# Another form of seven products in gate/up and feature transform, and one more product made jointly

## The chip, the cores and the metric

The kernel runs on one core of a Trainium2 chip. The metric is the device time of one execution in microseconds (us), taken as the median of several runs. Five engines work side by side, each through its own stream of instructions in order: TensorE (PE in the profile; PEld is its weight load), VectorE (DVE), ScalarE (ACT), GpSimd (POOL), which here only starts transfers, and SyncE (SP), which starts most of the loads. Transfers run on 16 DMA engines. TensorE adds up its results in eight PSUM banks.

## The reference

The input x has 2048 rows of 512 in float32. Two branches are mixed by a gate g, one number a row.

```python
# A: the real part of a two-dimensional Fourier transform, by matrices
a = einsum("bsd,ed->bse", x, dft_hid_re)
b = einsum("bsd,ed->bse", x, dft_hid_im)
A = einsum("ts,bse->bte", dft_seq_re, a) - einsum("ts,bse->bte", dft_seq_im, b)
# B: a gated unit with 1792 hidden features
gate = einsum("bsd,df->bsf", x, W_gate)
up   = einsum("bsd,df->bsf", x, W_up)
B = einsum("bsf,fd->bsd", gate * (gate > 0) * up, W_down)

g = sigmoid((x * gate_w).sum(-1, keepdims=True))
return g * A + (1 - g) * B
```

## The kernel before

**Products.** Every float32 operand is split into a high and a low part: ScalarE casts it to the high part (names ending in h), VectorE subtracts that from the original for the low part (ending in l). A product of two matrices is then three matmuls: high by low, low by high, high by high (`PARTS`). On top of that, 2 x 2 block products are done with seven half-size products instead of eight (Strassen, or Winograd's form of it), so the operands of a product are sums of blocks, made by VectorE, and the results are sums of products, made in PSUM or by VectorE and ScalarE.

**Two forms of seven products.** `LEFT`, `RIGHT`, `ORDER` and `BANK` (lines 25 to 30) describe the form that the gate/up blocks (`Block`, line 560) and the feature transform (`SpectralBlock`, line 734) use before: order 5, 2, 1, 3, 4, 6, 7 in three pairs of banks a, b, c. In `Block` bank c is begun by ScalarE with minus the content of a ("seed"), and product 1 is added on top; the other sums are made by VectorE on the way out. The stages `Round`, `Down`, `Sequence` and `Joint` use the other form already, in which banks called A, B (or E), X, D and G are begun by copies of other banks.

**Stages**, in the order of TensorE, where the plan's time is counted in "keys", one key for one matmul of 128 x 128 x 512:

1. `Direct`: the first block of gate/up without the form of seven, 96 keys; then 11 `Block`s of 84 keys. A `Block` makes 256 hidden features, gate and up, for one half of the rows (q). Its weights are prepared by `Weights`; its result h and sums of it are stored by `h_out` for later.
2. Four `SpectralBlock` stages of 84 keys (the two feature transforms, real and imaginary), with the last two `Block`s behind them.
3. `Down`, twice 294 keys: the down projection for both halves.
4. The sequence transform: a real matrix (m = 0) and an imaginary one (m = 1), each for two halves of the output rows (p). `Sequence(left, m, p)` makes those products that are not in `JOINT`, product by product, each in four parts (jj) of 12 matmuls. `Joint(m, of)` makes one product of the outer form for both halves of the columns and rows at once, with another level of the form of seven inside: seven products, each in two parts of 6 matmuls. `JOINT` before holds (0, 1), (0, 2), (0, 3) and (1, 2): matrix and outer product.

The stages of m = 0 leave their results in the scratch tensor zd; those of m = 1 begin from it: `Sequence.fill` loads z and ScalarE copies it into a bank before the products come. In each `Sequence` of m = 1 before, bank A is filled with z11, product 1 is added, VectorE makes bank B from z12 minus A (`seed`), and the later products are added there.

**Operands of the sequence transform.** `right_sums` loads four blocks of a transform matrix (tiles p), makes four sums on VectorE and stores them to the scratch tensor tb through GpSimd's queue. The table `SUMS` says which (matrix, outer product or 4 + p, part) are done so, and at which key; of 4 and 5 stand for the two `Sequence` halves. Joint stages and those parts of `Sequence` read the sums back (tiles jr and r from tb). Other parts load three blocks, make three sums on the spot and get the fourth by an accumulating transfer through GpSimd's queue. The tiles ch, cl (in joint stages jch, jcl) are the split right operands; lh, ll (jt) the split left ones.

**What sets the order.** All of this is written as steps with a key, and `Plan` orders them before the kernel is built: it models each step's length and each transfer, works out when each must be done (due), and lists the steps of each engine in the order in which they would start. VectorE's and ScalarE's steps go by due time and may not begin more than 40 keys ahead of their key. Buffers are 51 units of 4 KB per partition; a step whose unit isn't free yet has to wait. In the kernel on the chip every engine and queue then runs its list in order. PSUM banks are handed out in rotation, eight in all.

Of the kernel before, what the change touches and what calls it, by code (L numbers as in the profile page):

```python
# [24 lines left out]
LEFT = {1: ("11", "22", 1), 2: ("21", "22", 1), 3: ("11",), 4: ("22",), 5: ("11", "12", 1),  # L25
        6: ("21", "11", -1), 7: ("12", "22", -1)}
RIGHT = {1: ("11", "22", 1), 2: ("11",), 3: ("12", "22", -1), 4: ("21", "11", -1), 5: ("22",),
         6: ("11", "12", 1), 7: ("21", "22", 1)}
ORDER = (5, 2, 1, 3, 4, 6, 7)
BANK = {5: "a", 3: "a", 6: "a", 2: "b", 4: "b", 7: "b", 1: "c"}  # L30
# [59 lines left out]
class Step:  # L90


    def __init__(self, key, engine, name, a, k):
# [13 lines left out]
        if name == "tensor_copy":  # L107
            self.work = 0.1 + n * 0.52e-3
            self.hold = self.work - 0.05
        elif name == "dma_start":  # L110
            n = max(x.size() // (P if x.base.kind == "dram" else 1) for x in (*self.writes, *self.reads))
            self.work = n * 4 * P / 4096 * 0.160 / 16 * (2 if "accum_op" in k else 1)
        elif engine == "tensor":
            self.work = self.hold = 0.22667 * n / N
        elif engine == "vector":

            self.work = 0.163 + n * 1.0625e-3
            self.hold = self.work - 0.083
        else:
            self.work = 0.19 + n * 0.845e-3  # L120
            self.hold = self.work - 0.09
# [8 lines left out]
class Queues:  # L130
# [31 lines left out]
    def add(self, step, start):  # L162
# [5 lines left out]
        packets = max(1.0, step.work / (0.160 / 16 * (2 if "accum_op" in step.k else 1)))  # L168
# [176 lines left out]
def kernel(ctx: ExitStack, tc, xP, xG, wf, wgu, wd, cr, ci, wri, gw, out):  # L345
# [40 lines left out]
    wb = hbm("wb", 8, P, 4, 2, P)  # L386
# [61 lines left out]
    def x_raw(q, m):  # L448

        a, *r = RIGHT[m]  # L450
        raw = piece[q, {6: "12", 7: "21"}[m] if m in (6, 7) else a] if not r or m in (6, 7) else buf(f"xs{m}")
        X[q, m] = buf(f"xh{m}", dtype=F32R), buf(f"xl{m}", dtype=F32R), raw

    def x_sum(q, m):
        a, *r = RIGHT[m]
        if m == 6:
            E().vector.scalar_tensor_tensor(X[q, m][2].all, piece[q, a].all, -1.0, piece[q, r[0]].all,
                                            op0=OP.mult, op1=OP.subtract)
        elif r:
            combine(X[q, m][2].all, piece[q, a].all, piece[q, r[0]].all, r[1])  # L460
# [16 lines left out]
    SLOT = {5: 0, 1: 1, 2: 2, 7: 0, 3: 1, 4: 2, 6: 3}  # L477

    class Weights:
        def __init__(self, c):  # L480
            self.c = c
            self.raw = [buf(f"wr{i}", [4, 2, P]) for i in range(2)]
            self.sum = [buf(f"ws{i}", [3, 2, P]) for i in range(2)]
            self.a = [[buf(f"wa{i}{x}", [3, 2, P], F32R) for x in "hl"] for i in range(2)]
            self.b = [[buf(f"wb{i}{x}", [4, 2, P], F32R) for x in "hl"] for i in range(2)]

        def load(self, i):
            load(self.raw[i].all, wgu[self.c, i])

        def a_sum(self, i):  # L490
            r, o = self.raw[i], self.sum[i]
            E().vector.tensor_add(o[:, 0:3], r[:, 0:3], r[:, 1:4])
            E().scalar.copy(self.a[i][0].all, o.all)

        def a_lo(self, i):
            E().vector.tensor_sub(self.a[i][1].all, self.sum[i].all, f32(self.a[i][0].all))

        def b_sum(self, i):
            r = self.raw[i]
            E().vector.tensor_sub(r[:, 0:4:3], r[:, 0:2], r[:, 2:4])  # L500

        def b_hi(self, i):
            E().scalar.copy(self.b[i][0].all, self.raw[i].all)

        def b_lo(self, i):
            E().vector.tensor_sub(self.b[i][1].all, self.raw[i].all, f32(self.b[i][0].all))

        def keep(self, key):
            for n, t in enumerate(y for x in (self.a, self.b) for i in x for y in i):
                k = t.shape[0]  # L510
                op(key + 3 * n, lambda n=n, t=t, k=k: store(wb[n, :, :k], f32(t.all)))

        def fetch(self, key):
            for n, t in enumerate(y for x in (self.a, self.b) for i in x for y in i):
                k = t.shape[0]
                op(key + 6 * n, lambda n=n, t=t, k=k: load(f32(t.all), wb[n, :, :k]))

        def of(self, m, i):
            return [t[:, SLOT[m]] for t in (self.a if m in (5, 1, 2) else self.b)[i]]

    def w_prep(w, key, ahead=66):
        for i in range(2):
            op(key - ahead + 6 * i, w.load, i)
            op(key - 36 + 12 * i, w.a_sum, i)
            op(key - 30 + 12 * i, w.a_lo, i)
            op(key + 6 * i, w.b_sum, i)
            op(key + 6 * i, w.b_hi, i)
        op(key + 6, w.b_lo, 0)
        op(key + 12, w.b_lo, 1)
# [30 lines left out]
    class Block:  # L560


        def __init__(self, q, w):
            self.q, self.w = q, w
            self.t, self.g, self.u = buf("t"), buf("g"), buf("u")
            self.h = [buf(f"h{d}") for d in range(2)]
            self.ps = {k: Pair("c") for k in "abc"}
            for m in ORDER:
                for i in range(2):
                    pe(6, self.product, m, i)  # L570
                    self.evac(m, i, plan.now)
            h_out(q, w.c, self.h, plan.now + (8 if plan.now > 270 else 100))

        def product(self, m, i):
            w, x, ps = self.w.of(m, i), X[self.q, m], self.ps[BANK[m]]
            if m in (5, 2) and i == 0:
                ps.new()
            n = 0
            for k in range(2):
                for a, b in PARTS:  # L580
                    mm(ps[i], w[a][:, k], x[b][:, k], start=m in (5, 2) and n == 0, stop=n == 5)
                    n += 1

        def evac(self, m, i, key):
            a, b, c = (self.ps[k] for k in "abc")
            t, g, h = self.t, self.g, self.h

            def go():
                e = E()
                if m == 5:  # L590

                    if i == 0:
                        c.new()
                    e.scalar.activation(c[i], a[i], AF.Copy, scale=-1.0)
                elif m == 2:
                    e.scalar.copy(t[:, i], b[i])
                elif m == 1:
                    e.vector.tensor_sub(t[:, i], c[i], t[:, i])

                elif m in (3, 4):  # L600
                    j, ps = (0, a) if m == 3 else (1, b)
                    if i == 0:
                        e.scalar.activation(g[:, j], ps[0], AF.Relu)
                    else:
                        e.vector.tensor_mul(h[0][:, 1] if m == 3 else h[1][:, 0], g[:, j], ps[1])
                else:
                    j, ps, o = (0, a, h[1][:, 1]) if m == 6 else (1, b, h[0][:, 0])
                    u = self.u[:, j] if i == 0 else o
                    e.vector.tensor_add(u, ps[i], t[:, i])
                    if i:  # L610
                        e.vector.scalar_tensor_tensor(o, self.u[:, j], 0.0, o, op0=OP.max, op1=OP.mult)

            op(key, go)
# [99 lines left out]
    class Spectral:  # L713
# [8 lines left out]
        def prep(self, m, key):  # L722
            a, *r = LEFT[m]
            raw = self.raw[a] if not r or m in (6, 7) else buf(f"vs{m}")
            w = self.w[m] = buf(f"vh{m}", dtype=F32R), buf(f"vl{m}", dtype=F32R), raw
            if r:
                if m == 6:

                    a, r = r[0], (a, -1)
                op(key, lambda a=a, r=r: combine(raw.all, self.raw[a].all, self.raw[r[0]].all, r[1]))  # L730
# [3 lines left out]
    class SpectralBlock:  # L734
        def __init__(self, sp, q, ih):
            self.sp, self.q, self.ih = sp, q, ih
            self.t = buf("t")
            self.o = {b: buf("a" + b, (2, 2, HD)) for b in ("12", "21", "22", "11")}
            self.ps = {k: Pair("a") for k in "abc"}
            for m in ORDER:  # L740
# [3 lines left out]
                if m in (3, 4, 6, 7):  # L744
                    op(plan.now + 3, self.out, {3: "12", 4: "21", 6: "22", 7: "11"}[m])

        def product(self, m, i):
            x, w, ps = X[self.q, m], self.sp.w[m], self.ps[BANK[m]]
            first = m in (5, 2, 1)
# [9 lines left out]
        def evac(self, m, i):  # L759
            e, t = E(), self.t[:, i]  # L760
            a, b, c = (self.ps[k][i] if self.ps[k].banks else None for k in "abc")

            o = self.o[{3: "12", 4: "21", 6: "22", 7: "11"}[m]][:, :, i] if m in (3, 4, 6, 7) else None
            if o:
                a, b, t = (x and x.rearrange("p (k n) -> p k n", k=2) for x in (a, b, t))
            if m == 5:
                e.scalar.copy(t, a)
            elif m == 2:
                e.vector.tensor_add(t, t, b)
            elif m == 1:  # L770
                e.vector.tensor_sub(t, c, t)
            elif m == 3:
                e.scalar.copy(o, a)
            elif m == 4:
                e.scalar.activation(o, b, AF.Copy, scale=-1.0)
            elif m == 6:
                e.vector.scalar_tensor_tensor(o, a, -1.0, t, op0=OP.mult, op1=OP.subtract)
            elif m == 7:
                e.vector.tensor_add(o, b, t)
# [184 lines left out]
    class Sequence(Round):  # L964
        HI, LO = 31, 24

        def __init__(self, left, m, p):
            self.m, self.p, self.early = m, p, 0 if m else 40
            self.ORDER = tuple(x for x in ((1, 7, 6, 5, 4, 3) if m else (1, 5, 6, 7, 4)) if (m, x) not in JOINT)
            self.NEW = () if m else (1, 5, 7)  # L970
            if m:
                self.g = gate_row((2 * p, 2 * p + 1), plan.now + 10)
                self.z = {b: buf("z") for b in ("11", "22", "12")}
                for b, key in zip(self.z, (76, 110, 60)):
                    op(plan.now - key + 48 * (b != "11"), lambda b=b: load(self.z[b].all, zd[self.place(b)]))
# [16 lines left out]
        def rights(self):  # L992
# [5 lines left out]
            for jj in range(4):  # L998
# [9 lines left out]
                for b, t in (("12", 110), ("22", 105), ("11", 90 if m else 100)):  # L1008
                    x = (1 if b == "11" else 7) if m else 5
# [462 lines left out]
```

## Time and profile before

| | before |
|---|---|
| time, median of 3 runs | 783.41 us (783.38 to 784.32) |
| profiled execution, first to last instruction (its span) | 782.1 us |
| TensorE busy | 777.5 us, 3428 matmuls |
| VectorE busy | 698.4 us, 795 instructions |
| ScalarE busy | 406.2 us, 537 instructions |
| moved by DMA | 248.41 MB, 318 GB/s in the mean |

The profiled execution has no time of its own beside its span; the runs' times also hold what lies around the span. Busy time of an engine is the time in which any instruction of it ran. A matmul lasts longer than the distance to the next one, since they overlap; the distance is what counts for a sum. The helper `Step.run` records every operation, so all rows have the same line, L127; groups are told apart by the names of tiles. The DMA share is the time that packets took, as a share of 16 engines, and can pass 1.

### The profile page before, as it was taken

How to read it: one execution, taken by the hardware profiler on the slowest of the kernel's cores; microseconds unless marked ns; L12 is line 12 of the kernel's file. 1: busy time of each engine (PE TensorE's matmuls, PEld its weight loads, DVE VectorE, ACT ScalarE, POOL GpSimd, SP SyncE). 2: the span in 40 equal slices, each digit the busy share in tenths (PEclk: the TensorE clock that was granted, in tenths of full speed). 3: DMA queues.
4: the chain of work that ended last, by engine and by line, in shares of the span. 5: the costliest groups of instructions: out<-in, count | busy, mean ns of one | idle time of the engine just before them, and what ended most of it. 6: DMA issues, size and time to landing. Idle time of an engine off the chain costs nothing.

```text
span 782.1 us, 9936 instructions
## 1 busy us (share of the span) xinstructions
PE 777.5 (99%) x3428; PEld 644.0 (82%) x3428; DVE 698.4 (89%) x795; ACT 406.2 (52%) x537; POOL 115.2 (15%) x181
## 2 busy tenths in 40 slices
PE   9999999999999999999999999999999999999998
PEld 7888888888888888888888888888888888888886
DVE  6999999999999654899997799987999999989896
ACT  5643322222234112464656576576679857645762
POOL 0101322232222112011110000100100002012010
PEclk9999999999999999999999999999999999999999
DMA  8623999999996699589999999989999998997954
GB/s 318 259 95 121 324 404 414 418 325 419 419 396 199 230 338 419 219 302 382 415 417 408 380 313 359 310 281 343 331 390 412 410 358 206 325 238 217 327 156 108
DMA packets 71891, 248.41 MB, mean 318 GB/s; under 512 B 8224, under 2 KB 8992, under 8 KB 71840
## 3 DMA queue, kind: packets, MB, share of 16 engines
q1 hardware_dynamic: 47360, 159.02, 54.1%
q0 software_dynamic: 24336, 88.62, 33.6%
q8 instruction: 27, 0.44, 0.2%
q14 instruction: 24, 0.20, 0.1%
q10 hardware_dynamic: 144, 0.13, 0.1%
HBM read 165.94 MB, written 81.80 MB: 317 GB/s over the span
## 4 chain that ended last, share of the span: by engine, by line
PE 99%; ACT 0%; issue 0%; DVE 0%; ACTq 0%
PE z L127 45%; PE c L127 35%; PE a L127 10%; PE jB L127 3%; PE jA L127 3%; PE jX L127 1%; PE jD L127 1%; PE jG L127 1%; PE warm L127 0%; PE jH L127 0%; ACT jo L127 0%; DVE warm L127 0%; ACTq L127 0%
## 5 line engine op out<-in xcount | busy, mean ns | idle before, releaser
L127 PE MATMUL z<-ch,ll 128*128 128x512 f32 x516 | 200.7, 389 | 0.0
L127 PE MATMUL z<-cl,lh 128*128 128x512 f32 x516 | 200.7, 389 | 0.0
L127 PE MATMUL z<-ch,lh 128*128 128x512 f32 x516 | 200.7, 389 | 0.0
L127 PEld LDWEIGHTS z<-ch,lh 128*128 128x128 f32 x516 | 96.9, 188 | 20.2
L127 PEld LDWEIGHTS z<-ch,ll 128*128 128x128 f32 x516 | 96.9, 188 | 20.0
L127 PEld LDWEIGHTS z<-cl,lh 128*128 128x128 f32 x516 | 96.9, 188 | 20.0
L127 ACT CAST ch<-r 128x1024 fp32r<-128x1024 f32 x80 | 82.5, 1053 | 57.3 <-DVE r L127 43.1
L127 DVE TENSOR_TENSOR cl<-r,ch 128x1024 fp32r<-128x1024 f32 x80 | 96.3, 1220 | 8.2 <-ACT ch L127 6.4
L127 DVE TENSOR_TENSOR cl<-hr,ch 128x1024 fp32r<-128x1024 f32 (+1 forms) x56 | 60.1, 1087 | 11.8 <-ACT ch L127 7.5
L127 DVE TENSOR_TENSOR jcl<-jr,jch 128x1024 fp32r<-128x1024 f32 x56 | 67.2, 1221 | 3.4 <-PE z L127 1.5
L127 ACT CAST ch<-hr 128x1024 fp32r<-128x1024 f32 (+1 forms) x56 | 52.0, 945 | 31.6 <-DMA hr<-hd 11.1
L127 ACT CAST jch<-jr 128x1024 fp32r<-128x1024 f32 x56 | 57.7, 1054 | 5.3 <-DVE jcl L127 2.5
L127 DVE TENSOR_TENSOR p<-p,p 128x1024 f32<-128x1024 f32 x44 | 53.4, 1220 | 0.3
L127 DVE TENSOR_TENSOR r<-r,r 128x1024 f32<-128x1024 f32 x39 | 47.0, 1219 | 3.5 <-DMA r<-cr 3.5
L127 ACT ACTIVATE c<-c 128x512 f32<-128x512 f32 x26 | 15.1, 582 | 66.8 <-PE c L127 66.8
L127 ACT COPY z<-z 128x512 f32<-128x512 f32 x56 | 31.6, 586 | 21.2 <-PE z L127 18.7
L127 PE MATMUL c<-xh,wb0l 128*128 128x512 f32 x104 | 40.5, 389 | 0.0
L127 PE MATMUL c<-xl,wb0h 128*128 128x512 f32 x104 | 40.5, 389 | 0.0
L127 PE MATMUL c<-xh,wb0h 128*128 128x512 f32 x104 | 40.5, 389 | 0.0
L127 PE MATMUL c<-xh,wb1l 128*128 128x512 f32 x104 | 40.5, 389 | 0.0
L127 PE MATMUL c<-xl,wb1h 128*128 128x512 f32 x104 | 40.5, 389 | 0.0
L127 PE MATMUL c<-xh,wb1h 128*128 128x512 f32 x104 | 40.5, 389 | 0.0
(237 smaller groups left out, 1541.1 us busy)
## 6 DMA issues: line engine op xcount, KB each, us to landing
tb<-p POOLq DMA_DIRECT2D x44, 512.0 KB, 10.1
hr<-hd SPq DMA_DIRECT2D x42, 512.0 KB, 9.2
p<-cr SPq DMA_DIRECT2D x36, 512.0 KB, 7.7
jr<-tb SPq DMA_DIRECT2D x32, 512.0 KB, 9.1
hd<-hs POOLq DMA_DIRECT2D x28, 512.0 KB, 8.1
r<-ci SPq DMA_DIRECT2D x24, 512.0 KB, 8.7
l<-ad SPq DMA_DIRECT2D x20, 512.0 KB, 8.7
jr<-cr SPq DMA_DIRECT2D x18, 512.0 KB, 8.8
```

The source lines that it names most:

```text
L127: getattr(getattr(nc, self.engine), self.name)(*map(ap, self.a), **{k: ap(x) for k, x in self.k.items()})
```

## The change

- `Block` and `SpectralBlock` take the form of seven products that the later stages use, in the order 1, 5, 6, 2, 7, 3, 4, with five pairs of banks A, B, X, D, G. ScalarE begins X from A (negated in `Block`), D from X and G from D; it copies B to y and X to s; VectorE adds these to banks B and D on the way out. The weights of gate and up are laid out so that one tile holds both, and their sums and splits follow the new form.
- Product 1 of matrix 1 goes into a joint stage with product 1 of matrix 0: `Joint((0, 1), 1)` runs over four parts (both matrices, two each) and adds all of them up in the same banks. Both `Sequence` stages of m = 1 lose product 1; what they need of it comes in z11 from zd, and z12 minus z11 is made by VectorE ahead of the stage and copied into bank B by ScalarE.
- `SUMS` gets 16 entries instead of 11, at other keys: the two parts of (1, 1) and four more parts of the `Sequence` stages of m = 1 are added, one of m = 0 is taken out.
- The plan's model of transfers takes 0.166 for 0.160 and an accumulating transfer as 1.6 instead of 2 plain ones.

```diff
-ORDER = (5, 2, 1, 3, 4, 6, 7)
-BANK = {5: "a", 3: "a", 6: "a", 2: "b", 4: "b", 7: "b", 1: "c"}
+ORDER = (1, 5, 6, 2, 7, 3, 4)
+BANK = {1: "A", 2: "A", 5: "B", 3: "B", 6: "X", 7: "D", 4: "G"}
...
-            self.work = n * 4 * P / 4096 * 0.160 / 16 * (2 if "accum_op" in k else 1)
+            self.work = n * 4 * P / 4096 * 0.166 / 16 * (1.6 if "accum_op" in k else 1)
...
     def w_prep(w, key, ahead=66):
...
+        for n in range(2):
+            op(key - ahead + 6 * n, w.load, n)
+        for m, n, k in ((None, 0, -40), (5, None, -36), (6, 2, -30), (7, 1, -12), (3, 3, 0)):
+            if m:
+                op(key + k, w.sum, m)
+            if n is not None:
+                op(key + k + 2, w.hi, n)
+                op(key + k + 8, w.lo, n)
...
-    JOINT = ((0, 1), (0, 2), (0, 3), (1, 2))
-    SUMS = {(0, 5, 0): 420, (0, 3, 0): 485, (0, 3, 1): 550, (0, 1, 0): 615, (0, 1, 1): 680, (0, 2, 0): 745,
-            (0, 2, 1): 810, (1, 2, 0): 875, (1, 2, 1): 940, (0, 5, 1): 1640, (0, 4, 1): 1720}
+    JOINT = ((0, 1), (0, 2), (0, 3), (1, 1), (1, 2))
+    SUMS = {(0, 5, 0): 160, (0, 3, 1): 150, (0, 1, 1): 330, (1, 2, 0): 465, (0, 1, 0): 535, (1, 5, 2): 637, (0, 5, 1): 680, (1, 1, 1): 715, (0, 2, 1): 790, (0, 3, 0): 955, (1, 1, 0): 995, (1, 2, 1): 1150, (0, 2, 0): 1270, (1, 5, 1): 1564, (1, 5, 3): 1929, (1, 4, 0): 377}
...
     class Block:
...
+        def evac(self, m, i):
+            e, p, h = E(), self.ps, self.h
+            def seed(k, j, scale=1.0):
+                if i == 0:
+                    p[k].new()
+                e.scalar.activation(p[k][i], p[j][i], AF.Copy, scale=scale)
+            if m == 1:
+                seed("X", "A")
+            elif m == 5:
+                e.scalar.copy(self.y[:, i], p["B"][i])
+            elif m == 6:
+                seed("D", "X")
+                e.scalar.copy(self.s[:, i], p["X"][i])
+            elif m == 7:
+                seed("G", "D")
+            if m in (2, 4):
+                o, ps = (h[0][:, 0], p["A"]) if m == 2 else (h[1][:, 0], p["G"])
+                if i == 0:
+                    e.scalar.activation(self.g[:, m // 4], ps[0], AF.Relu)
                 else:
+                    e.vector.tensor_mul(o, self.g[:, m // 4], ps[1])
+            elif m in (3, 7):
+                o, ps, t = (h[0][:, 1], p["B"], self.s) if m == 3 else (h[1][:, 1], p["D"], self.y)
+                e.vector.tensor_add(t[:, 0] if i == 0 else o, ps[i], t[:, i])
+                if i:
+                    e.vector.scalar_tensor_tensor(o, t[:, 0], 0.0, o, op0=OP.max, op1=OP.mult)
...
     class Sequence(Round):
...
-            self.NEW = () if m else (1, 5, 7)
+            self.NEW = () if m else (5, 7)
...
-                for b, key in zip(self.z, (76, 110, 60)):
+                for b, key in zip(self.z, (76, 110, 98)):
                     op(plan.now - key + 48 * (b != "11"), lambda b=b: load(self.z[b].all, zd[self.place(b)]))
-                for k, b, key in (("A", "11", -14), ("D", "22", 20)):
+                op(plan.now - 16, lambda: combine(self.z["12"].all, self.z["12"].all, self.z["11"].all, -1))
+                for k, b, key in (("D", "22", -14), ("B", "12", -6)):
                     op(plan.now + key, self.fill, k, self.z[b])
             super().__init__(left, (2, 2, 2, 2))
+            if m:
+                self.o["11"] = self.z["11"]
+                self.done("11", self.base + 40)
...
-            if x == 1:
-                op(key, seed)
-                op(key + 1, lambda: both(copy, o["11"], a))
-                self.done("11", key + 6)
...
     class Joint:
...
-        def __init__(self, m, of, last=False):
+        def __init__(self, ms, of, last=False):
...
-            self.lefts(self.base - (60 if last else 80), 10)
-            for jj in range(2):
-                self.rights(jj)
+            for n, m in enumerate(ms):
+                self.lefts(m, self.base - (60 if last else 80) + 4 * n, 10 * len(ms))
+            for j in self.parts:
+                self.rights(*j)
...
-                    for jj in range(2):
-                        pe(6, self.product, x, jj)
+                    for j in self.parts:
+                        pe(6, self.product, x, j)
...
-    Joint(0, 3)
-    for x, key in zip((1, 7, 6, 5, 4, 3), (30, 80, 376, 410, 450, 490)):
+    Joint((0,), 3)
+    for x, key in zip((7, 6, 5, 4, 3), (80, 376, 410, 450, 490)):
...
     Sequence(lefts[0], 0, 1)
-    Joint(0, 1)
-    Joint(0, 2)
+    Joint((0, 1), 1)
+    Joint((0,), 2)
     Sequence(lefts[1], 1, 1)
     Sequence(lefts[1], 1, 0)
-    Joint(1, 2, True)
+    Joint((1,), 2, True)
```

More of the change, by code (lines that the diff above doesn't have):

```diff
@@ L481, in __init__ @@
             self.c = c
[L482 to L506, printed above, removed]
+            self.raw = [buf(f"wr{n}", [4, 2, P]) for n in range(3)] + [buf("wr3", [2, 2, P])]
@@ new lines, in __init__, with load, sum @@
+            self.w = [[buf(f"w{n}{x}", [4, 2, P], F32R) for x in "hl"] for n in range(3)]
+            self.w3 = buf("w3", [4, 2, P], F32R)
+        def load(self, n):
+            load(self.raw[n].all, wgu[self.c, n])
+        def sum(self, m):
+            x, y, z, v = self.raw
+            o, a, b = {5: (z[:, :2], y[:, 2:], y[:, :2]), 7: (y[:, 2:], x[:, :2], y[:, 2:]),
+                       6: (z[:, 2:], z[:, :2], x[:, :2]), 3: (v.all, x[:, 2:], z[:, 2:])}[m]
+            (E().vector.tensor_add if m == 5 else E().vector.tensor_sub)(o, a, b)
@@ L508, in keep, with part, hi, lo @@
+        def part(self, n, x):
+            return self.w[n][x].all if n < 3 else self.w3[:, 2 * x:2 * x + 2]
+        def hi(self, n):
+            E().scalar.copy(self.part(n, 0), self.raw[n].all)
+        def lo(self, n):
+            E().vector.tensor_sub(self.part(n, 1), self.raw[n].all, f32(self.part(n, 0)))
+        def parts(self):
+            return [y for x in self.w for y in x] + [self.w3]
         def keep(self, key):
[L509 to L511 removed]
+            for n, t in enumerate(self.parts()):
+                op(key + 3 * n, lambda n=n, t=t: store(wb[n], f32(t.all)))
@@ L513, in fetch @@
         def fetch(self, key):
-            for n, t in enumerate(y for x in (self.a, self.b) for i in x for y in i):
-                k = t.shape[0]
-                op(key + 6 * n, lambda n=n, t=t, k=k: load(f32(t.all), wb[n, :, :k]))
+            for k, n in enumerate((0, 1, 4, 5, 2, 3, 6)):
+                op(key + 6 * k, lambda n=n: load(f32(self.parts()[n].all), wb[n]))
         def of(self, m, i):
-            return [t[:, SLOT[m]] for t in (self.a if m in (5, 1, 2) else self.b)[i]]
+            n, f = SLOT[m]
@@ L521, in w_prep @@
+            return [(self.w[n][x] if n < 3 else self.w3)[:, 2 * f + i + (2 * x if n == 3 else 0)] for x in range(2)]
     def w_prep(w, key, ahead=66):
[L522 to L529, printed above, removed]
-    JOINT = ((0, 1), (0, 2), (0, 3), (1, 2))
@@ L580, in product @@
                 for a, b in PARTS:
-                    mm(ps[i], w[a][:, k], x[b][:, k], start=m in (5, 2) and n == 0, stop=n == 5)
+                    mm(ps[i], w[a][:, k], x[b][:, k], start=m in (1, 5) and n == 0, stop=n == 5)
                     n += 1
[L584 to L605, printed above, removed]
-                else:
[L607 to L613, printed above, removed]
@@ L1175, in new, with product @@
             self.b[k] = Buf(plan, "j" + k, [N], kind="bank")
-        def product(self, x, jj, k=None, columns=slice(None)):
-            first = x in ((1, 7, 5, 4) if self.last else (1, 5)) and jj == 0 and k is None
+        def product(self, x, j, k=None, columns=slice(None)):
+            begin, end = j == self.parts[0], j == self.parts[-1]
+            first = x in ((1, 7, 5, 4) if self.last else (1, 5)) and begin and k is None
             k = k or {1: "A", 2: "A", 7: "D", 6: "X", 4: "G"}.get(x, "B")
@@ L1181, in product @@
                 self.new(k)
-            c = self.c[x, jj]
+            c, t = self.c[x, *j], self.t[x, j[0]]
             for i in range(2):
                 for n, (a, b) in enumerate(PARTS):
-                    mm(self.b[k][:, columns], self.t[x][:, a, 2 * jj + i], c[b][:, i, columns],
-                       start=first and i == n == 0, stop=jj == i == 1 and n == 2)
+                    mm(self.b[k][:, columns], t[:, a, 2 * j[1] + i], c[b][:, i, columns],
+                       start=first and i == n == 0, stop=end and i == 1 and n == 2)
         def halves(self, h):
-            for jj in range(2):
-                self.product(4, jj, f"H{h}", HALVES[h])
+            for j in self.parts:
+                self.product(4, j, f"H{h}", HALVES[h])
         def evac_on(self, x, key):
```

141 lines of the change are left out of this document (68 added, 73 removed).

## The prediction

> **What bounds the kernel now.** First the page and the list of who waited for whom on TensorE.
>
> ```profile
> span 782.1 us, 9936 instructions
> PE 777.5 (99%) x3428; PEld 644.0 (82%) x3428; DVE 698.4 (89%) x795; ACT 406.2 (52%) x537; POOL 115.2 (15%) x181
> DMA packets 71891, 248.41 MB, mean 318 GB/s; under 512 B 8224, under 2 KB 8992, under 8 KB 71840
> PE warm L127 <- DVE warm L127: 1.1, 1, 1.1
> ```
>
> TensorE's only listed wait is 1.1 us at the start. So the span is a count of matmuls, and only two things can move it: another count, or a first wait. The chain of waits, in order of time, gives the price of a matmul and the stages.
>
> ```profile
> 237.13 76.16 PE a L127 x336
> ...
> 528.17 2.72 PE jA L127 x12
> ...
> 547.21 43.52 PE z L127 x192
> 590.73 2.72 PE jA L127 x12
> ...
> 609.77 2.72 PE jA L127 x12
> ...
> 626.09 2.72 PE jG L127 x12
> 628.81 130.56 PE z L127 x576
> ```
>
> 43.52 / 192 = 0.2267 us a matmul. The feature transform's four stages (a tiles) end at 237.13 + 76.16 = 313.3. Joint stages (j tiles) start at 528.17, 590.73 and 609.77; 84 matmuls make one, 19.04 us. The 576 of z are the two Sequence stages of the second matrix, 288 each. Next the busy time stage by stage, cut at these times; columns: window, length, then busy time and count on PE, PEld, DVE, ACT, POOL, the granted clock, DMA share, GB/s.
>
> ```profile
> 27.69:46.73 19.04, 19.04 (x85) 15.77 (x85) 19.00 (x23) 10.59 (x14) 1.59 (x3) 1.00 0.23 91
> 199.05:218.09 19.04, 19.04 (x85) 15.77 (x85) 17.74 (x21) 4.59 (x7) 5.11 (x9) 1.00 1.03 420
> 418.01:484.65 66.64, 66.64 (x295) 55.20 (x295) 57.57 (x55) 44.23 (x55) 2.13 (x4) 1.00 0.96 366
> 484.65:528.17 43.52, 43.52 (x193) 36.05 (x193) 40.50 (x41) 28.17 (x36) 5.36 (x8) 1.00 0.89 290
> 528.17:547.21 19.04, 19.04 (x85) 15.77 (x85) 14.05 (x13) 13.13 (x18) 0.53 (x1) 1.00 0.94 346
> 547.21:590.73 43.52, 43.52 (x193) 36.05 (x193) 43.18 (x44) 32.53 (x41) 4.56 (x6) 1.00 1.04 366
> 590.73:609.77 19.04, 19.04 (x85) 15.77 (x85) 18.95 (x22) 19.04 (x26) 0.59 (x2) 1.00 1.03 410
> 609.77:628.81 19.04, 19.04 (x85) 15.77 (x85) 18.48 (x20) 15.41 (x23) 1.45 (x3) 1.00 1.02 409
> 628.81:694.09 65.28, 65.28 (x289) 54.07 (x289) 61.48 (x57) 41.70 (x52) 7.33 (x9) 1.00 0.96 283
> 694.09:759.37 65.28, 65.28 (x289) 54.07 (x289) 59.85 (x59) 41.91 (x52) 7.68 (x9) 1.00 0.86 244
> ```
>
> Behind a perfect TensorE three others are nearly full from 547 to 629 us: DVE 80.6 of 81.6 us, ACT all of 19.04 in the first joint stage there, and the DMA share above 1. A full DMA reads 1.02 to 1.04 in this view, so I take 1.03 as its capacity.
>
> **The change, part by part.**
>
> *Matmuls.* A Sequence stage of the second matrix spends 4 x 12 = 48 matmuls on each product (288 / 6). Product 1 leaves both: minus 96. The joint stage for output 1 now has four parts of 6 matmuls for each of seven products, 168 where it had 84: plus 84. Net minus 12, times 0.2267: **minus 2.72 us**. The other form of seven products has the same matmul count in every block. This is the one term on the path.
>
> *Blocks (13) and feature transform (4 stages).* Of each Block's evacuations, DVE has 8 instructions for 10 and ACT 12 for 6; of each transform stage's, DVE 4 for 8 and ACT 14 for 6. One of each kind, with its mean:
>
> ```profile
> L127 DVE TENSOR_TENSOR t<-c,t 128x512 f32<-128x512 f32 x26 | 17.4, 684 | 0.3 <-ACT wa0h L127 0.3
> L127 ACT ACTIVATE c<-c 128x512 f32<-128x512 f32 x26 | 15.1, 582 | 66.8 <-PE c L127 66.8
> ACT c L127 <- PE c L127: 66.8, 23, 7.6
> ACT ch L127 <- DVE r L127: 43.1, 23, 4.4
> L127 ACT CAST jch<-jr 128x1024 fp32r<-128x1024 f32 x56 | 57.7, 1054 | 5.3 <-DVE jcl L127 2.5 <-DVE jr L127 1.1 <-DVE jt L127 0.6
> ```
>
> DVE loses 13 x 2 + 4 x 4 = 42 x 0.684 = 28.7 us; ACT gains 13 x 6 + 4 x 8 = 110 x 0.58 = 64 us, and had 376 us idle. The new waits are seeds: ACT copies bank A into X, X into D, D into G, and a later product adds on top. From a half-product's last matmul to the first matmul that needs its seed lie three other half-products, 18 x 0.2267 = 4.08 us, as for the one seed (c from a) that each Block has already; behind a late seed stand all later matmuls, since TensorE takes them in order, and on ACT the next weight casts. Cost nothing as long as ACT is free within 3.5 us. Five pairs of banks instead of three go round in eight, so a block's second A bank waits for DVE's reading of the last block's first B bank; 24 x 0.2267 = 5.44 us lie between, against 4.08 us for today's tightest DVE read. Bounds: 0 to some 2 us a miss; no gain is possible, for TensorE does not wait there. I take 0. The weights' and x's splits change by a few DVE instructions, less in all; they are covered as the present ones are.
>
> *Block sums written ahead.* There are 16 such groups for 11, each of 4 loads, 4 DVE sums and 4 stores on POOL's queue, and they begin at key 150 instead of 420, where the DMA share is 0.23.
>
> ```profile
> L127 DVE TENSOR_TENSOR p<-p,p 128x1024 f32<-128x1024 f32 x44 | 53.4, 1220 | 0.3
> tb<-p POOLq DMA_DIRECT2D x44, 512.0 KB, 10.1
> 591.96 0.69 DVE L127 TENSOR_TENSOR jn<-jl,jl 128x512 f32<-128x512 f32 x1
> 592.57 4.69 DVE L127 TENSOR_TENSOR jcl<-jr,jch 128x1024 fp32r<-128x1024 f32 x4
> ...
> 619.56 1.22 DVE L127 TENSOR_TENSOR jcl<-jr,jch 128x1024 fp32r<-128x1024 f32 x1
> 620.70 3.49 DVE L127 TENSOR_TENSOR cl<-r,ch 128x1024 fp32r<-128x1024 f32 x3
> ```
>
> Instructions overlap: three take 3.49, so a wide one costs DVE (3.49 - 1.22) / 2 = 1.135 us, a 512-wide one 0.61 (592.57 - 591.96). Five groups more: 20 x 1.135 = 22.7 us of DVE, paid by the 28.7 freed, and 40 transfers, 21.0 MB. Loads go on SP's queue, past weight loads due every second block; stores on POOL's, ahead of the h stores that the Down stages read far later. Cost 0 while they fit the early hole; if not, see the second rival.
>
> *The joint stage with both matrices.* Today's joint stage needs of DVE 14 jcl x 1.135 + 11 left sums and splits x 0.61 + 2 additions x 0.61 = 23.8 us in 19.04, so it eats a lead of 4.8. With both matrices: 28, 22 and 2, 46.4 us in 38.08. The rise is 22.6 us of DVE against 19.04 of TensorE: 3.6 us of lead more. What is there? The last jcl of today's pair ends at 619.56 + 1.22 = 620.78 and is first read half way through the jG product, at 626.09 + 1.36 = 627.45: 6.7 us. 3.1 would be left, and the 5.0 us that DVE idles from 528 to 547 can be drawn on. ACT is alike: 28 casts for 14, with 11.0 us idle from 547 to 591. Stall 0; bounds 0 to 3.6 + (what is lost of 6.7).
>
> Behind it, the second matrix's stages lose 8 cl and 2 left splits, and for four of eight parts the 3 sums made on the spot: 22 x 1.135 = 25 us off DVE. The wait for product 1 and its DVE seed is replaced by a load of z, one subtraction and fills by ACT ahead of the stage. One part of the first matrix goes back to sums on the spot: 3.4 us of DVE where 3.0 are idle and 5.0 follow.
>
> *DMA from 484.65 to 759.37.* Share times length: 38.7 + 17.9 + 45.3 + 19.6 + 19.4 + 62.7 + 56.1 = 259.7 us. Queues from 628.81 to 694.09, then the DMA row in 40 slices from 694.09 to 759.37:
>
> ```profile
> q1 hardware_dynamic: 3965, 13.69, 54.3%
> q0 software_dynamic: 1296, 4.72, 41.6%
> DMA  9989950863499997999999999999999999558500
> ```
>
> A plain 0.524 MB costs 0.524 x 0.543 x 65.28 / 13.69 = 1.36 us; q0's nine, nearly all accumulating, 27.2 / 9 = 3.0 us. Added: 14 jr and 2 jl loads, less 2 left loads: 14 x 1.36 = 19.0. Four parts take 5 loads for 3 and an accumulation: 4 x (2 x 1.36 - 3.0) = -1.1. The part that goes back: 3.0 - 1.36 = +1.6. Sum 279.2; capacity 1.03 x 272.0 = 280.2. But the last six slices leave 6.0 us idle (0.5, 0.5, 0.2, 0.5, 1 and 1 of 1.63), since the last stage's data is in by then. So 5.0 us must go ahead of 484.65, where the stage from 418.01 has (1.03 - 0.96) x 66.64 = 4.7. It fits, barely. I take 0.
>
> The traffic grows by 40 x 0.524 = 21.0 MB for the sums, 14 x 0.524 = 7.3 for these loads and 4 x 0.524 = 2.1 for the four parts: 248.4 + 30.4 = 278.8 MB. The row from 199.05 has 420 GB/s for a whole stage, and at that rate this is 664 us; the rest of the span is room for accumulations.
>
> A rule of the Trainium skill speaks against the change: "DMA: Bandwidth & Descriptors", section Bandwidth, says that a core's share of HBM, about 358 GB/s, binds HBM-SBUF transfers, and not the fabric at 435. By that page my estimate for the same traffic would be 779 us of DMA. The rows from 199.05, 590.73 and 609.77, at 409 to 420 GB/s, do not agree with it.
>
> **The sum.** 782.1 - 2.72 = 779.4 of span. The median lies 783.41 - 782.1 = 1.31 above the profiled span; kept, this gives 783.41 - 2.72 = **780.7 us**. About 0.2% (1.6 us) is what a measurement of this kernel can tell from no change, so faster means under 781.8 and slower above 785.0.
>
> **The rivals.**
>
> *The vector engine's lead is used up.* For: DVE is 99% busy for 81.6 us ahead of 629, and the change asks 22.6 us more in a stretch 19.04 longer. Against: the 6.7 us of lead. If that lead and the 1.0 us idle are all there is, and 6.7 cannot be used because buffers (51 units of 4 KB, of which two matrices' left sides hold about twice as many) keep casts from running ahead, TensorE waits 22.6 - 19.04 - 1.0 = 2.6 us: 783.3, no change.
>
> *The DMA becomes the bound in the last third* (the slower side). Place: 531 to 757 us, where SP's queue is in order, so that one late load holds all behind it. If nothing goes ahead of 484.65, the wait is 279.2 + 6.0 - 280.2 = 5.0 us: 785.7; with capacity 1.00 instead of 1.03 it is 13.2: 793.9. It decides once more than 2.7 us of transfers come too late, and is slower above 4.3. For: four stages read 1.02 to 1.04 already. Against: today DMA in those stages brings r loads for 629 onward, so it runs well ahead.
>
> *Seeds come late.* ACT stood up to 4.4 us behind one DVE result; such a stand plus a cast of 1.05 and the seed of 0.58 would miss 4.08 by 1.95 us. Three such misses in 13 blocks give 786.6. Against: the 4.4 was in a stage of r tiles, and the first seed of each Block has had the same 4.08 without one wait.
>
> *Memory does not sustain the rate.* If the added traffic pulled the mean of the program down to the 366 GB/s of the row from 547.21, 278.8 MB would take 762 us, and with a last joint stage of 19.04 and the end, 3.7, in which nothing is left to load, 784.5 + 1.3 = 785.8. Against: that row holds accumulating transfers, and plain stages read 409 and more. By the Trainium skill's page named above, with 358, it would be 803 as an estimate.
>
> That the change does not remove the 12 matmuls can be excluded: they are counted from its loops.
>
> **How the numbers follow.** Forecast 780.7: 0.61. Vector lead 783.3: 0.12. DMA bound from 785.7: 0.18. Late seeds: 0.07, in part under 785.0 and a little still faster. Memory rate: 0.02. Faster 0.62, same 0.14, slower 0.24. The range begins at 780.2 (the forecast and the lowest of the runs) and reaches to 787.0, into the DMA case; 2 in 10 are left out, mostly above.
>
> **What would show it.** Right: 3416 matmul records, no new row among TensorE's waits, seven joint products of 5.44 us between 591 and 629, Sequence stages of 54.4 us each. The DVE lead at the end of the following joint stage should be near 3 us. Wrong: TensorE waiting for jcl near 640 (first rival), for loads through casts after 629 (second), or for X, D or G banks between 28 and 313 (third). A DMA share that still has holes at 30 to 85 us would say that the early sums did not fill them.

## The result and the profile after

| | before | after |
|---|---|---|
| time, median of 18 runs each | 783.57 us (782.73 to 784.75) | 784.72 us (783.97 to 786.90) |
| ratio to before | | 1.0017 (95% interval 1.0010 to 1.0024) |
| matmuls | 3428 | 3416 |
| span of the profiled run | 782.1 us | 785.0 us |

The 12 matmuls are gone, and yet the kernel is 0.17% slower. The profiled run after is one of four among the 18 that took 786.5 to 786.9 us with a mean granted clock of 0.997 or 0.998, where the other fourteen lie at 784.0 to 785.3; what sets them apart is seen below.

The page of the changed kernel, and behind it its list of TensorE's waits (who waited for whom: us in total, times, longest):

```profile
span 785.0 us, 10154 instructions
PE 777.0 (99%) x3416; PEld 642.2 (82%) x3416; DVE 684.4 (87%) x773; ACT 466.1 (59%) x653; POOL 122.8 (16%) x197
DMA packets 80213, 278.83 MB, mean 355 GB/s; under 512 B 9120, under 2 KB 9888, under 8 KB 80160
```

```profile
PE c L123 <- ACT c L123: 2.5, 1, 2.5
PE warm L123 <- DVE warm L123: 1.1, 1, 1.1
PE z L123 <- ACT z L123: 0.3, 1, 0.3
PE z L123 <- DVE cl L123: 0.2, 1, 0.2
```

There is one new wait of size: once, for an instruction of ScalarE that writes a bank c from a bank c, a seed. TensorE's busy time is longer than 3416 matmuls need (777.0, where 777.5 - 2.72 = 774.8 was to be expected), so some matmuls were slow as well. TensorE in order of time shows both:

```profile
33.73 0.39 PE L123 MATMUL c<-xh,w2h 128*128 128x512 f32 x1
36.62 0.53 PE L123 MATMUL c<-xh,w2l 128*128 128x512 f32 x1 [2.50 <-ACT c L123]
36.95 0.62 PE L123 MATMUL c<-xl,w2h 128*128 128x512 f32 x1
37.37 0.63 PE L123 MATMUL c<-xh,w2h 128*128 128x512 f32 x1
...
39.93 0.59 PE L123 MATMUL c<-xb21h,w0h 128*128 128x512 f32 x1
40.36 0.40 PE L123 MATMUL c<-xb21h,w0l 128*128 128x512 f32 x1
```

Between the starts at 33.73 and 36.62 lie 2.89 us where 0.23 is the rule: 2.66 lost. The next nine steps, to 40.36, take 3.74 us instead of 2.04: another 1.70. The row of that stretch in the view by windows has the granted clock in the column before the DMA share:

```profile
36.62:40.36 3.74, 3.74 (x9) 2.92 (x10) 3.34 (x5) 3.43 (x7) 1.58 (x3) 0.54 0.55 222
```

Half the clock, right behind the wait. ScalarE and SP's queue, in order of time, say why the seed was late:

```profile
30.44 0.58 ACT L123 ACTIVATE c<-c 128x512 f32<-128x512 f32 x1
35.03 1.04 ACT L123 CAST w0h<-wr 128x1024 fp32r<-128x1024 f32 x1 [4.01 <-DMA wr<-wgu]
35.98 0.58 ACT L123 ACTIVATE c<-c 128x512 f32<-128x512 f32 x1
```

```profile
14.26 4.83 SPq L123 DMA_DIRECT2D p<-cr  x5
20.05 0.33 SPq L123 DMA_DIRECT2D wr<-wgu  x1
21.32 2.25 SPq L123 DMA_DIRECT2D p<-cr  x2
25.73 0.33 SPq L123 DMA_DIRECT2D wr<-wgu  x1
```

The first seed of bank X begins at 30.44. Behind it in ScalarE's list stands the cast of a weight tile of the next block (c = 2), and only behind that the second seed. The load of these weights is issued at 20.05, behind five loads for the early sums, and lands 15.0 us later, at 35.0. In the kernel before, SP's queue has nothing but weight loads in that stretch:

```profile
13.46 37.77 SPq L127 DMA_DIRECT2D wr<-wgu  x4
```

In the changed kernel ScalarE stands still for 4.01 us with a seed behind it whose source is ready. The Trainium skill, "Perfetto Trace Analysis", section Per-instruction lifecycle, says that ScalarE, VectorE and GpSimd take their instructions strictly in order; the trace agrees, with these 4.01 us.

From 41 us to the last third nothing is lost: in the chain of waits the transform's 336 matmuls begin at 241.15 for 237.13 before, and the joint stage of both matrices at 594.75 for 590.73, both 4.02 later. That is less than 2.66 + 1.70 = 4.36, because the first matmuls of the profiled run after took some 0.35 us less than those of the run before. The chain's later rows:

```profile
241.15 76.16 PE a L123 x336
...
594.75 5.44 PE jA L123 x24
...
632.83 2.72 PE jA L123 x12
...
761.90 2.72 PE jA L123 x12
```

From 632.83 to 761.90 are 84 + 480 = 564 matmuls, 127.85 us, and 129.07 went by: 1.2 us lost, with the two small waits for a fill of z and for a low part cl in it. From 761.90 to the end of the span it is 0.37 us longer than before. In sum -2.72 + 4.02 + 1.2 + 0.37 = +2.9, by which the spans differ.

The medians come out of the same terms without the half clock, which most runs did not have: -2.72 + 2.66 + 1.2 = +1.1, and 784.72 - 783.57 = 1.15.

### The profile page after: what moved, and what is told of

Read it like the earlier page. It is cut to its first block, busy times and chain, and to the rows that moved or that the text cites. A ratio compares the mean times of both kernels' runs of the same rounds, so it can differ in the third digit from the quotient of the medians.

```text
span 785.0 us, 10154 instructions
## 1 busy us (share of the span) xinstructions
PE 777.0 (99%) x3416; PEld 642.2 (82%) x3416; DVE 684.4 (87%) x773; ACT 466.1 (59%) x653; POOL 122.8 (16%) x197
## 2 busy tenths in 40 slices
DMA packets 80213, 278.83 MB, mean 355 GB/s; under 512 B 9120, under 2 KB 9888, under 8 KB 80160
## 4 chain that ended last, share of the span: by engine, by line
PE 86%; DMA 5%; issue 4%; DVE 3%; ACT 0%; SPq 0%; POOL 0%; DVEq 0%; POOLq 0%; ACTq 0%
PE z L123 35%; PE c L123 31%; PE a L123 10%; PE jB L123 3%; PE jA L123 3%; DMA x<-xP 2%; DMA wr<-wgu 2%; PE jX L123 2%; PE jD L123 1%; DMA out<-z 1%; PE jG L123 1%; DVE r L123 1%; DVE cl L123 1%; DVE jcl L123 1%; SPq L123 0%
## 5 line engine op out<-in xcount | busy, mean ns | idle before, releaser
L123 DVE TENSOR_TENSOR p<-p,p 128x1024 f32<-128x1024 f32 x64 | 77.1, 1220 | 10.6 <-DMA p<-ci 8.6
L123 DVE TENSOR_TENSOR jcl<-jr,jch 128x1024 fp32r<-128x1024 f32 x70 | 83.6, 1219 | 2.0 <-ACT jch L123 1.9
L123 ACT ACTIVATE c<-c 128x512 f32<-128x512 f32 x78 | 45.6, 585 | 63.0 <-PE c L123 50.2
L123 POOL DMA_DIRECT2D tb<-p x64 | 35.0, 546 | 126.2 <-DVE p L123 115.2
L123 PE MATMUL c<-xh,w2l 128*128 128x512 f32 x104 | 40.8, 393 | 2.5 <-ACT c L123 2.5
L123 PE MATMUL c<-xh,w2h 128*128 128x512 f32 x104 | 40.9, 394 | 0.0
L123 PE MATMUL c<-xl,w2h 128*128 128x512 f32 x104 | 40.9, 394 | 0.0
L123 PE MATMUL c<-xh,w1l 128*128 128x512 f32 x104 | 40.5, 389 | 0.0
L123 PE MATMUL c<-xl,w1h 128*128 128x512 f32 x104 | 40.5, 389 | 0.0
L123 PE MATMUL c<-xh,w1h 128*128 128x512 f32 x104 | 40.5, 389 | 0.0
```

What stands on the lines that cost most here:

```text
L123: getattr(getattr(nc, self.engine), self.name)(*map(ap, self.a), **{k: ap(x) for k, x in self.k.items()})
```

## The experiments

**The weight load ahead of the sums' loads.** Theory: one late load holds a cast, and the cast holds the seed. Rival: the early sums fill the DMA, and something else comes late instead.

```diff
-                    w_prep(w, plan.now, 66 if c else 180)
+                    w_prep(w, plan.now, 90 if c == 2 else 66 if c else 180)
```

> The changed kernel, but the two weight loads of block c = 2 have key 90 and 96 instead of 114 and 120, so they stand ahead of the seven loads for the first two groups of sums on SP's queue. Theory (one late load: it holds ScalarE's cast of these weights, and behind the cast stands the second seed of bank X): the 2.5 us wait of TensorE at 34 us and the 1.7 us at half clock behind it are gone, the feature transform begins near 237.1 us as before, and the time is 784.7 - 2.7 = 782.0 us where the clock had held, up to 4.3 less where it had dropped; about 0.2% under the kernel before. Rival (the early sums fill the DMA engines, so something else comes late in the weights' place, such as the sums' own loads on VectorE ahead of a bank's reading): a wait of 2 us or more remains between 28 and 60 us, time 784 to 785.

Measured: 782.03 us, ratio 0.9980 (0.9972 to 0.9989). SP's queue, ScalarE, and TensorE's waits:

```profile
14.02 1.60 SPq L123 DMA_DIRECT2D wr<-wgu  x2
16.59 11.10 SPq L123 DMA_DIRECT2D p<-cr  x8
```

```profile
30.71 1.03 ACT L123 CAST w0h<-wr 128x1024 fp32r<-128x1024 f32 x1
31.65 0.58 ACT L123 ACTIVATE c<-c 128x512 f32<-128x512 f32 x1
```

```profile
PE warm L123 <- DVE warm L123: 1.1, 1, 1.1
PE c L123 <- ACT wf0h L123: 0.5, 1, 0.5
PE z L123 <- ACT z L123: 0.3, 1, 0.3
```

The cast stands ahead of the second seed as it did, but its weights are there, and the seed comes 4.3 us earlier. The wait and the half clock are gone, and no wait of more than 0.5 us took their place (that one, for wf0h, stands at the very start). The theory holds.

**The sums' loads later, the weight load where it was.** The same from the other side.

```diff
-    SUMS = {(0, 5, 0): 160, (0, 3, 1): 150, ...
+    SUMS = {(0, 5, 0): 210, (0, 3, 1): 200, ...
```

> The changed kernel with the first two groups of sums at keys 210 and 200 instead of 160 and 150; the weight loads of block c = 2 keep their keys 114 and 120 and so go out ahead of the sums' loads. Theory (it is these loads ahead of the weights): the same as with the early weight load, 782.0 us, without TensorE's wait near 34 us, though the sums themselves come later. Rival (the early hole in the DMA has to be used from key 150 on, or the 20 us of transfers are missing later): new waits of TensorE between 60 and 313 us, 783 or more.

Measured: 782.01 us, ratio 0.9984 (0.9975 to 0.9992), and TensorE's only waits are those at the start and the 0.3 us for z. So it is the order of these loads. The stores of the two groups' sums are issued at 49.2 to 60.7 us, against 37.1 to 51.7 with the early weight load; that costs nothing.

**The weight load still later.** The dose, with the lists of all other engines kept.

```diff
+        late = [s for s in self.steps if s.engine == "sync" and s.key in (114, 120)]
+        sums = [s for s in self.steps if s.engine == "sync" and s.key in (100, 106, 110, 116, 118, 128)]
+        self.steps = [s for s in self.steps if s not in late]
+        n = self.steps.index(sums[-1]) + 1
+        self.steps[n:n] = late
         at = {s: n for n, s in enumerate(self.steps)}
```

> The changed kernel with the lists of all engines as they are, except that on SP's queue the two weight loads of block c = 2 stand behind all eight early sum loads instead of behind five and seven. Theory (ScalarE waits for this load, and TensorE's wait follows it one for one): the weights land 3 x 0.524 MB / 0.417 MB per us = 3.8 us later, near 38.8 us, TensorE's wait grows from 2.5 to about 6.3 us, the time from 784.7 to about 788.5, and the half clock behind the wait is seen in every run. Rival (the wait has another cause that only ends at the same time): no change by more than 1 us.

Measured: 790.28 us, ratio 1.0085 (1.0072 to 1.0099). ScalarE and TensorE's waits:

```profile
38.27 1.04 ACT L123 CAST w0h<-wr 128x1024 fp32r<-128x1024 f32 x1 [8.24 <-DMA wr<-wgu]
39.22 0.58 ACT L123 ACTIVATE c<-c 128x512 f32<-128x512 f32 x1
```

```profile
PE c L123 <- ACT c L123: 5.8, 1, 5.8
```

The cast begins at 38.27 instead of 35.03, 3.24 us later, and TensorE's wait grows from 2.50 to 5.75, by 3.25: one for one. The weights came 0.6 us earlier than the 3.8 expected. The time rose by 5.6 rather than 3.8. In the trace the nine steps behind the wait, from 39.85 to 43.73, took 3.88 us instead of 2.04, 1.84 lost at the lower clock; all four runs had a mean clock of 0.995 or 0.996, so it seems that every one paid this, as four of 18 did before. 3.25 + 1.84 = 5.1; the last 0.5 us are not explained.

**The cast later instead of the load earlier.** Is it the order on ScalarE?

```diff
+                late = 14 if w.c == 2 and n == 0 else 0
-                op(key + k + 2, w.hi, n)
-                op(key + k + 8, w.lo, n)
+                op(key + k + 2 + late, w.hi, n)
+                op(key + k + 8 + late, w.lo, n)
```

> The changed kernel with all loads where they were; only the cast and the low part of the first weight tile of block c = 2 have keys 14 later, so that the cast stands behind both seeds of X in ScalarE's list. Theory (what costs is the order on ScalarE): the weights still land near 35 us, ScalarE still waits for them, but TensorE does not: 782.0 us as with the early load. Rival (the DMA's lateness itself costs): TensorE waits 2 us or more for the weights or for what stands behind the cast, 784 to 785.

Measured: 784.40 us, ratio 1.0011 (1.0002 to 1.0020). The expectation of the theory failed; the rival's time came, with a wait of 1.88 us. The profiled run is the slowest of the eleven, 785.83. ScalarE, VectorE and TensorE in order of time:

```profile
30.92 0.58 ACT L123 ACTIVATE c<-c 128x512 f32<-128x512 f32 x1
34.98 1.05 ACT L123 CAST w0h<-wr 128x1024 fp32r<-128x1024 f32 x1 [2.97 <-DMA wr<-wgu]
...
39.31 0.69 DVE L123 TENSOR_TENSOR wr<-wr 128x512 f32<-128x512 f32 x1 [2.02 <-DMA wr<-wgu]
...
53.43 1.04 ACT L123 CAST w1h<-wr 128x1024 fp32r<-128x1024 f32 x1 [5.12 <-DVE wr L123]
54.38 0.58 ACT L123 ACTIVATE c<-c 128x512 f32<-128x512 f32 x1
...
55.02 0.50 PE L123 MATMUL c<-xh,w2l 128*128 128x512 f32 x1 [1.88 <-ACT c L123]
```

The wait at 34 us is gone, as the theory says: both seeds are done before ScalarE stands still. But VectorE stands twice instead: 2.44 us ahead of 36.06 for the result of this cast, whose low part it has to make, and 2.02 us ahead of 39.31 for the second weight load, which is late too. VectorE's list then runs behind, at 53.43 a cast has waited 5.12 us for one of its sums, and the seed behind that cast is late in the next block. So the order on ScalarE decides where the lateness bites; the lateness of the two loads is the cause, and has to be taken away at SP's queue. That these two stands are what reaches 53 us is read from the order of VectorE's list, not tried by itself.

**The other form alone.** The changed `Block`, `SpectralBlock`, `Weights` and what prepares x, with the sums table, joint and sequence stages of before.

```diff
-ORDER = (5, 2, 1, 3, 4, 6, 7)
+ORDER = (1, 5, 6, 2, 7, 3, 4)
...
     JOINT = ((0, 1), (0, 2), (0, 3), (1, 2))
```

> The kernel before with the other form of seven products in blocks and feature transform alone: sums table, joint stages, sequence stages and the model of transfers are those of before; 3428 matmuls. Theory (the form is free where no load stands ahead of a seed): no new wait on TensorE, 783.6 us, within 0.1% of before; VectorE busy about 29 us less, ScalarE about 64 more. Rival (seeds by ScalarE are late by themselves, or the rotation of ten banks in eight costs): waits on ACT c or on banks in several of the 13 blocks, 786 or more.

Measured: 783.93 us, ratio 1.0002 (0.9993 to 1.0011). The page's line of engines and TensorE's waits:

```profile
PE 776.7 (99%) x3428; PEld 643.1 (82%) x3428; DVE 664.2 (85%) x749; ACT 462.8 (59%) x646; POOL 114.5 (15%) x180
```

```profile
PE warm L123 <- DVE warm L123: 1.1, 1, 1.1
```

VectorE has 698.4 - 664.2 = 34 us less and ScalarE 57 more, where 29 and 64 were expected, and TensorE waits for no seed and no bank. The form costs nothing by itself: here no early sums stand ahead of the weights.

**The joint stage alone.** The changed sums table, joint and sequence stages, with the old form in blocks and transform.

```diff
 ORDER = (5, 2, 1, 3, 4, 6, 7)
...
-    JOINT = ((0, 1), (0, 2), (0, 3), (1, 2))
+    JOINT = ((0, 1), (0, 2), (0, 3), (1, 1), (1, 2))
```

> The kernel before with the joint stage of both matrices, the sums table and the sequence stages of the changed kernel, but the old form in blocks and feature transform and the old model of transfers; 3416 matmuls. Theory (the form of the blocks pays for the sums): VectorE, with 23 us more of sums and nothing freed, is late with bank readings and weight parts from 80 to 115 us, and TensorE waits 5 to 13 us: 786 to 794. Rival (the sums fit without the other form): 781 to 782.5.

Measured: 795.30 us, ratio 1.0150 (1.0136 to 1.0164), 1.3 us beyond the range of the theory. TensorE's longest waits and one stretch by windows:

```profile
PE c L127 <- DMA wb1l<-wb: 1.8, 1, 1.8
PE c L127 <- DVE wb1l L127: 1.8, 2, 1.2
PE c L127 <- DVE h L127: 1.5, 2, 0.8
PE c L127 <- DVE wb0l L127: 1.0, 1, 1.0
```

```profile
85.00:104.00 19.00, 15.42 (x62) 10.84 (x61) 18.84 (x25) 5.95 (x9) 6.33 (x10) 1.00 0.93 352
```

VectorE is busy for 18.84 of 19.00 us and TensorE for 15.42: with the sums on top and nothing freed, VectorE is the bound of the block stage. The longest single wait is another thing: 1.83 us for a load of a weight part (wb1l), at 334 us. So the two parts of the change belong together with this table of sums: one is free and gains nothing, the other needs what the first frees. Whether other keys would let the joint stage pay with the old form was not tried.

**Retimed.** The early weight load, left sides of joint stages 20 keys earlier, and other keys for the sums.

```diff
-                    w_prep(w, plan.now, 66 if c else 180)
+                    w_prep(w, plan.now, 90 if c == 2 else 66 if c else 180)
...
-                self.lefts(m, self.base - (60 if last else 80) + 4 * n, 10 * len(ms))
+                self.lefts(m, self.base - (60 if last else 100) + 4 * n, 10 * len(ms))
...
-    SUMS = {(0, 5, 0): 160, (0, 3, 1): 150, (0, 1, 1): 330, (1, 2, 0): 465, ... (1, 5, 1): 1564, (1, 5, 3): 1929, (1, 4, 0): 377}
+    SUMS = {(0, 5, 0): 160, (0, 3, 1): 189, (0, 1, 1): 300, (1, 2, 0): 525, ... (1, 5, 1): 1543, (1, 5, 3): 1794, (1, 4, 0): 407}
```

> The changed kernel with the early weight load, the left sides of joint stages begun 20 keys earlier (base - 100 instead of base - 80), and the keys of the 16 groups of sums moved by up to 135 until the plan's model shows no wait of TensorE over 0.1 us behind the start. Theory (what is left of the loss after the early load is VectorE's lead behind the three joint stages: 0.6 us at the fill of bank B near 654 us): that wait is gone too, 782.0 - 0.7 = 781.3 us, where 783.57 - 2.72 = 780.85 would be the full gain. Rival (the DMA in the last third is what runs out): waits for loads appear there, 782 or more.

Measured: 781.15 us, ratio 0.9970 (0.9959 to 0.9981): the fastest of all, under both kernels. Its waits:

```profile
PE warm L123 <- DVE warm L123: 1.1, 1, 1.1
PE c L123 <- ACT wf1h L123: 0.8, 1, 0.8
```

The wait for z is gone, and no load in the last third took its place; the 0.8 us for wf1h stand at 10.9 us, at the first weights. Which of the two further edits did it was not tried apart.

## Why the prediction was wrong, point by point

**Matmuls: right.** 3416, and the stages have the lengths that were worked out (5.44 us a joint product). Without the late waits the kernel gains 783.53 - 781.15 = 2.4 of the 2.72 us. The 1.31 us between median and span compare two different executions: in each of the 18 runs after, the time lies 1.7 to 1.9 us above its own span. The forecast of 780.7 doesn't hang on it.

**Seeds and sums: here the prediction failed.** Two terms that were put at 0 make up the miss: 784.72 - (783.57 - 2.72) = 3.9 us, of which 2.66 are the late seed and 1.2 VectorE's lead (below). The larger step is the sentence on the early sums, "Cost 0 while they fit the early hole", and with it "I take 0" for the seeds. It had named that their loads pass the weight loads on SP's queue, and did not follow it: who casts these weights, and what stands behind that cast. And the hole was not where the loads went. The prediction took the mean share of 0.23 from 27.69 to 46.73. In finer windows, three rows of the kernel before and then one of the changed kernel:

```profile
18.00:24.00 6.00, 6.00 (x28) 4.98 (x27) 6.00 (x8) 4.08 (x6) 2.17 (x4) 1.00 1.04 417
30.00:33.50 3.50, 3.50 (x17) 2.90 (x16) 3.50 (x4) 2.18 (x4) 0.43 (x1) 1.00 1.00 391
33.50:36.70 3.20, 3.20 (x16) 2.65 (x15) 3.20 (x5) 1.76 (x3) 0.00 (x0) 1.00 0.11 45
```

```profile
30.00:33.50 3.50, 3.50 (x17) 2.88 (x16) 3.46 (x5) 1.02 (x2) 0.00 (x0) 1.00 1.03 420
```

In the kernel before, the DMA was full from 18 to 24 us and again from 30 to 33.5; the long hole began at 33.5. The loads with key 100, some 27 us in the plan's count, were issued from 14.26 on, as soon as SP came to them, into a DMA that was full already. The hole filled only in part: from 46.73 to 60 us the share rose from 0.44 to 0.68, and from 60 to 85 from 0.46 to 0.71.

**The third rival named the mechanism and was given 0.07.** It asked for a ScalarE that stands 4.4 us with a seed behind it, priced a miss at 1.95 us, and put it aside because that stand had been seen with r tiles only. What it had wrong is whom ScalarE waits for: not a result of VectorE but a load. The stand was 4.01 us, the miss 2.66, once and not three times; 1.70 us at half clock, which no term of the sum had, came on top in the profiled run. The measured 784.7 lies near the 785.7 of the DMA rival, but by luck: in the stretch that this rival named, TensorE waited for no load.

**VectorE's lead: the place was right, "Stall 0" was not.** Of the lead, 3.1 us were to be left. The last jcl of the stage from 632.83 ends at 647.73 + 1.22 = 648.95 and is first read at 632.83 + 6.5 x 2.72 = 650.51:

```profile
647.73 1.22 DVE L123 TENSOR_TENSOR jcl<-jr,jch 128x1024 fp32r<-128x1024 f32 x1
...
655.73 1.22 DVE L123 TENSOR_TENSOR z<-z 128x1024 f32<-128x1024 f32 x1
```

1.6 us. The prediction had the new subtraction of z ahead of the stage and gave it no time. VectorE, with no pause after 639.5, came to it only at 655.73, 3.9 us into the stage that begins at 651.87, and the fill of bank B behind it made TensorE wait. It was not a load: the last one of z was issued at 642.0, and none of the three took more than 11.3 us. This wait and the one for cl are in the 1.2 us lost there; the rival's price of 2.6 was too high.

**The DMA's budget: right.** 278.83 MB moved, for 278.8 worked out. The changed kernel's stages from 551.23 to 651.87:

```profile
551.23:594.75 43.52, 43.52 (x193) 36.04 (x193) 40.74 (x41) 32.99 (x41) 4.59 (x6) 1.00 1.04 366
594.75:632.83 38.08, 38.08 (x169) 31.53 (x169) 38.08 (x44) 35.62 (x47) 0.53 (x1) 1.00 1.03 409
632.83:651.87 19.04, 19.04 (x85) 15.77 (x85) 18.72 (x21) 13.45 (x19) 1.07 (x2) 1.00 1.03 411
```

Full for 100 us, and TensorE waited for no load there. The prediction held these rates against the Trainium skill without a condition that stands in the same section of "DMA: Bandwidth & Descriptors", Bandwidth: about 358 GB/s is what each core gets when both cores of the pair stream, and a single core was measured at 425. The 409 and 411 GB/s of this one core agree with that; no run here has a second core streaming.

## What to carry to other kernels

A transfer that is moved into an idle stretch is a change to every load behind it on its queue: find what was queued there, who waits for it, and what stands behind that waiter on its own in-order engine. Read idle DMA time from windows as fine as the transfers, and from the issue times in the trace rather than from the plan's keys. Where an engine starts banks for TensorE, no instruction that can wait for a transfer should stand between a bank's source and its seed, or its transfer should be early beyond doubt.

## What was not expected of the hardware

A wait of 2.50 us, and one of 1.88 in the experiment with the later cast, were followed by some 3 us at half clock: matmuls of 512 columns stood 0.43 us apart instead of 0.227, and each of the two waits cost 1.70 us more. By the mean clocks it did not come in every run: in four of 18 of the changed kernel, whose trace has the wait of 2.5 us, and in all four of the kernel whose trace has 5.8. In the experiment with the joint stage alone, the waits of up to 1.22 us in the stretch shown left the clock at 1.00, and so did the one of 1.83 us at 334 us. The Trainium skill, "TensorE: Matmul & The Clock Gate", section HAM oscillation, warns of idle gaps over about 3.4 us; here shorter ones were enough. The same page has the activity window run freely, not started by the kernel, which would fit that it depends on the run; no run here shows the window itself.
